# Delta rule, then a hash-routed mixture of experts: halves, fills and an order of loads

## The chip, the cores and the metric

The kernel runs on one core of a Trainium2 chip. The engines named here are TensorE (PE; its weight loads are PEld), VectorE (DVE), ScalarE (ACT), GpSimd (POOL) and SyncE (SP), which issues most DMAs. The metric is the device time of one execution in microseconds, lower is better.

## The reference

Two stages follow each other. The first is a delta rule over 4 batches, 8 heads, 768 steps and a head dimension of 48:

```python
k_n = k / (np.linalg.norm(k, axis=-1, keepdims=True) + 1e-06)
state = np.zeros((B, H, D, D))
for t in range(S):
    kt, vt, bt = (k_n[:, :, t], v[:, :, t], beta[:, :, t, None])
    y[:, :, t] = np.einsum('bhd,bhde->bhe', q[:, :, t], state)
    v_old = np.einsum('bhde,bhd->bhe', state, kt)
    state = state + bt[:, :, :, None] * np.einsum('bhd,bhe->bhde', kt, vt - v_old)
```

Its output, seen as 3072 tokens of 8 x 48 = 384 numbers, goes to the second stage. A hash of the token's id picks one of 8 experts, and each expert is a feed-forward layer with a ReLU between:

```python
expert_idx = token_ids * np.int64(2654435761) % np.int64(E)
for e in range(E):
    mask = expert_idx == e
    out[mask] = np.maximum(x[mask] @ w1[e], 0.0) @ w2[e]      # 384 -> 1024 -> 384
```

All numbers are float32.

## The kernel before

**Phase 1** works on 24 chunks of 32 steps (`NU`, `C`), with all batches and heads side by side. Four chunks make a group (`GC`). For each group the transposed keys and queries (`turn`, L457) give Gram matrices (`gram`, L483; `first_gram`, L525, for the first group). VectorE inverts them step by step: `inverse`, whose 31 steps are a product (L624) and a sum (L622), and which starts with a transpose of the Gram matrices (L584). `turn_back` (L638) transposes the result, and `spread_t` and `masks_of` make the stationary matrices `Tz` and `MT` out of it: on ACT (L550), or on DVE (L544) from chunk `LATE` = 20 on.

The chunks themselves are a chain, `chunk(c)`:

- `scale_v` makes V1 on DVE (L569).
- TensorE multiplies the state by the keys (`ask`, L659) into the PSUM bank `psX`. V1 minus this is R. Up to chunk 19 TensorE first puts -V1 into the bank (L690, with `minus`, a negated identity) and ACT copies the sum out with its sign turned (L695); from chunk 20 DVE subtracts (L699).
- `solve` (L709) multiplies R by Tz, and ACT copies the result, W, out (L723).
- `update` (L738) adds the keys times W to the state in the banks `psS`, and the state is copied to SBUF for the next chunk (`renew`: L762 on ACT, L764 on DVE).
- `answer` (L779) and a second `ask` with the queries make the chunk's rows in `psY`; ACT copies them out (L788), and POOL scatters them to `x_scratch` in DRAM, sorted by expert (`store`, L794).

From chunk `TAIL` on (20 of 0 to 23) a chunk is split: heads 0 to 3 stay in `psX`, heads 4 to 7 go to the bank `z1` (`zs[1]`), R and W are made in two parts, and the copy of the state is shared by ACT (batches 0 and 1) and DVE (batches 2 and 3).

**The order of the instructions** on each engine is fixed when the program is built. Each piece of work is a `task` with an engine, an estimated time, what it reads and writes, and the banks it claims. `order()` is a list scheduler: it walks through the tasks by estimated time and takes the ready one with the longest estimated rest. It also keeps an account of when TensorE's instructions are fetched, by counting their words:

```python
for m in range(issued // BLOCK, (issued + t["words"]) // BLOCK + 1):   # BLOCK = 256
    if m == len(begun):
        if m > 1:
            have = max(have, begun[-1])
            have += BUSY_FETCH if have < BUSY else FETCH               # 4600 or 3800 ns
        begun.append(max(s, have))
    s = max(s, begun[m])
```

Where it expects TensorE to be idle, `fill()` puts matmuls of the identity by itself into a bank that is unused when the gap begins (L1192), up to four blocks of 128 columns in one instruction, for gaps of over 380 ns in the first 80 us of the plan. Everything with its order fixed waits in it: a later instruction of an engine can't pass an earlier one that isn't ready.

**The first expert** (two blocks of 128 rows and a late one, `first_expert`: L1041, L1052, L1065, L1075) is scheduled by the same planner, as work for idle time. The late block's hidden values, `h_late`, lie in `xqs[0]`.

**Phase 2** goes through the other seven experts in the order `RANKS`. For each of them `fetch` asks SP for the rows (`load_x`, L100, and `load_numbers`, L104) into one of two tiles `xqs`, by turns; `turn` transposes them on DVE (L108); `gemm1` (L1226) has eight outputs that use four banks by turns and are evicted by ACT (L1229) and DVE (L1231) alternately; `gemm2_turned` (L1263) or `gemm2` (L1242) follows, and POOL scatters the result (L1252). Weights come by `load_w` (L94, L117) into a pool with two places, or for the second expert by `load_w_parts` (L94, L125). The transposes of the next expert's rows stand between the evictions of the present one. Before the loop SP is told: the second expert's rows, its weights, the third expert's weights, and the third expert's rows. Those rows go into `xqs[0]`, where `h_late` has been.

Of the kernel before, what the change touches and what calls it, by code (L numbers as in the profile page):

```python
# [13 lines left out]
ACT = mybir.ActivationFunctionType  # L14
# [6 lines left out]
def kernel(  # L21
# [11 lines left out]
    nc = tc.nc  # L33
    P = 128
    B, H, S, D = q.shape
# [13 lines left out]
    RANKS = [4, 0, 1, 2, 3, 5, 6, 7]  # L49
# [38 lines left out]
    def expert_at(rank, engine):  # L88
        return value(AT_E + rank, engine, E - 1)
# [21 lines left out]
    def load_w(e, pool, eng):  # L111
        s2 = moe_w2[bass.ds(e, 1)].rearrange("o f d -> (o f) d")
        w1_sb = pool.tile([P, CO, F], F32, name="w1_sb")
        for part in w1_parts(e, w1_sb, eng):
            part()
        w2_sb = pool.tile([P, FO, DIN], F32, name="w2_sb")
        eng.dma_start(out=w2_sb, in_=s2.rearrange("(fo p) d -> p fo d", p=P))  # L117
        return w1_sb, w2_sb
# [39 lines left out]

    with ExitStack() as phase1:
        NU = S // C  # L160
        TAIL = NU - 4
        GC = 4
        NG = NU // GC
        HU = H // 2
# [88 lines left out]
        def task(eng, ns, reads, writes, emit, words=0, kb=0, more=0, boost=0, job=None,  # L253
                 hold=0, claim=(), slack=0, idle=False, release=()):
            deps = {writer[r] for r in reads if r in writer}
            for w in writes:
                deps |= readers.get(w, set())
                if w in writer:
                    deps.add(writer[w])
            i = len(tasks)  # L260
            deps.discard(i)
            tasks.append(dict(eng=eng, ns=ns, deps=deps, emit=emit, words=words, kb=kb,
                              more=more, boost=boost, job=job, hold=hold,
                              claim=claim, slack=slack, idle=idle, release=release))
            for r in reads:
                readers.setdefault(r, set()).add(i)
            for w in writes:
                writer[w] = i
                readers[w] = set()
            return i  # L270
# [15 lines left out]
        def order():  # L286
# [33 lines left out]
            def fill(i, idle, at):  # L320

                nonlocal issued
                rate = 1.67
                if at < 2000:

                    rate, idle = 3.34, idle - 900
                idle = min(idle, 2750 if at < 2000 else 1100)
                while idle > FILL_OVER and at < FILL_UNTIL:
                    unused = [b for b in range(len(homes)) if banks[b] is not None
                              and banks[b] <= at]  # L330
                    if not unused:
                        break
                    n = min(4, max(1, int((idle - 160) / (rate * P))))
                    fills.setdefault(i, []).append((unused[0], n))
                    issued += 2
                    idle -= n * rate * P
                    at += n * rate * P
# [17 lines left out]
            while len(done) < n:  # L355
# [8 lines left out]
                at, e = best  # L364
# [307 lines left out]
        def chunk(c):  # L672
# [10 lines left out]
            if c == 0:  # L683
                R, r_names = V1, ("V10",) * 2
            else:
                R_, V1_ = [t.rearrange("p h d -> p (h d)") for t in (R, V1)]
                by_pe = c < LATE
                if by_pe:

                    task("PE", 680, (f"V1{c % 2}",), ("psX",), lambda: nc.tensor.matmul(  # L690
                        flats[0], lhsT=minus, rhs=V1_, start=True, stop=True,
                        skip_group_check=True), words=2)
                ask(c, 0, xs, xn, xc, by_pe)
                if by_pe:
                    task("ACT", 420, ("psX",), r_names, lambda: nc.scalar.activation(  # L695
                        R_, flats[0], ACT.Copy, scale=-1.0))
                for i, part in enumerate(wide if split else ()):
                    task("DVE", 320, (xn[i], f"V1{c % 2}"), (f"R{i}",),
                         lambda i=i, part=part: nc.vector.tensor_tensor(  # L699
                             R_[:, part], V1_[:, part], flats[i][:, part], op=ALU.subtract))  # L700
# [502 lines left out]
    with tc.tile_pool(name="w_pool2", bufs=2) as w_pool2, \  # L1203
# [79 lines left out]
        def fetch(e):  # L1283
            cols, cw, blocks, xq = own(e)
            row = value(AT_ROW + e, mybir.EngineType.SP, N)
            load_x(row, blocks, xq, nc.sync)
            xns[e] = m_i.tile([P, KT], F32, name="numbers")
            load_numbers(row, cols, cw, xns[e][0:cw, 0:cols, None], nc.sync)
# [13 lines left out]
        with tc.manual_schedule():  # L1302
            fetch(RANKS[1])
            for part in parts:
                part()
            w_tiles[2] = load_w(expert_at(RANKS[2], mybir.EngineType.SP), w_pool2, nc.sync)
            fetch(RANKS[2])
            n_ov = nc.values_load(ov_i[0:1, NOV:NOV + 1], min_val=0, max_val=NOV)
            for c in range(CO):
                turn(RANKS[1], c)  # L1310
            for k in range(SC):
                send_rows(o_first[:, k], idx_i[:, k:k + 1], True)
            send_rows(o_late, idx_i[:, SC:SC + 1], True)
            for i, e in enumerate(RANKS):
                if e == FIRST:
                    continue
                w1_sb, w2_sb = w_tiles.pop(i)
                rest = [e for e in RANKS[i + 1:i + 3]]
                done = RANKS[i - 1] if RANKS[i - 1] in oTs else None

                def between(fo):

                    to = max(3, i + 1)
                    if fo == 0 and to < E and to not in w_tiles:
                        w_tiles[to] = load_w(expert_at(RANKS[to], mybir.EngineType.SP),
                                             w_pool if to == 4 else w_pool2, nc.sync)
                    elif fo == 1 and len(rest) > 1:
                        fetch(rest[1])
                    if fo % 2 and fo // 2 < CO and rest:
                        turn(rest[0], fo // 2)  # L1330
                    if fo % 2 and done is not None:
                        send(oTs[done], done, fo // 2)

                h_sb = m_h.tile([P, FO, CAP], F32, name="h_sb")
                gemm1(w1_sb, xTs.pop(e), h_sb, CAPS[e], between)
                if KTS[e] > CO:
                    oTs[e] = m_t.tile([P, CO, CAP], F32, name="oT")
                    for j in range(CO):
                        gemm2_turned(w2_sb, h_sb, oTs[e], j, CAPS[e])
                else:  # L1340
                    cols, cw, _, _ = own(e)
                    for j in range(cols):
                        gemm2(w2_sb, h_sb, j, cw, idx[e][0:cw, j:j + 1], True)
# [49 lines left out]
```

## Time and profile before

| | before |
|---|---|
| timed runs, median (lowest to highest) | 505.26 us (505.12 to 509.08) |
| profiled execution, device time | 498.96 us |
| its span, first to last instruction | 497.4 us |
| mean granted TensorE clock | 0.970 |
| PE, DVE, ACT, POOL busy | 459.2, 228.8, 191.7, 71.6 us |
| chunk 0's first solve / chunk 20's / last answer's end | 50.73 / 205.06 / 224.06 us |
| second expert's first matmul | 255.29 us |

The profile is one execution. A busy time is the union of the engine's instructions; matmuls are pipelined and their ends are modelled, so that a TensorE that is shown as busy can still have a little room. The granted clock is a share of full speed. In a row of the instructions in order of time, the first number is the start, the second the length, and a bracket at the end tells how long the engine had been idle and what released it. Where instructions of several kinds are merged, xN counts them; a matmul of float32 shows as two records.

### The profile page before, as it was taken

To read this page: it belongs to the slowest core of one execution; us is meant where nothing else is said; L and a number is where in the kernel's file an instruction comes from. 1 tells how busy PE (TensorE), PEld (TensorE's weight loads), DVE (VectorE), ACT (ScalarE), POOL (GpSimd) and SP (SyncE) were. 2 spreads that over 40 slices of the span, in tenths; PEclk is the share of its full clock that TensorE was granted. 3 is DMA by queue.
4 is the path that set the end of the run, shared out by engine and by line. 5 is a ranking of instruction groups with operands and counts; after the bars stand their busy time and mean duration, and the time that the engine had idled before them with its cause. 6 is when DMAs were issued, how large, how long until landed. Compare 5 with 4: busy or idle time off the path is not lost. (4 is left out here: it accounts for less than half of the span.)

```text
span 497.4 us, 15828 instructions
## 1 busy us (share of the span) xinstructions
PE 459.2 (92%) x6648; PEld 312.5 (63%) x6648; DVE 228.8 (46%) x720; ACT 191.7 (39%) x443; POOL 71.6 (14%) x106
## 2 busy tenths in 40 slices
PE   8882899999899899899998999999999999999990
PEld 6762677787687777787754555555555565655650
DVE  5799979998998889850102013012021130110100
ACT  4762779988698687441221011011011110100100
POOL 6000101202020022320020012113011022001010
PEclk9996699999999899999999999999999999999996
DMA  9997756679444447523999995645543016401010
GB/s 137 170 154 116 114 112 132 131 151 189 99 101 100 100 112 176 151 72 77 186 271 246 244 222 140 152 129 114 112 151 73 0 39 164 144 7 39 0 31 15
DMA packets 137180, 60.61 MB, mean 122 GB/s; under 512 B 123005, under 2 KB 131825, under 8 KB 137108
## 3 DMA queue, kind: packets, MB, share of 16 engines
q1 hardware_dynamic: 131572, 49.80, 49.6%
q0 software_dynamic: 5344, 9.66, 6.1%
q8 instruction: 53, 0.87, 0.8%
q10 hardware_dynamic: 192, 0.12, 0.2%
q14 instruction: 19, 0.16, 0.1%
HBM read 49.19 MB, written 10.42 MB: 120 GB/s over the span
## 5 line engine op out<-in xcount | busy, mean ns | idle before, releaser
L1263 PE MATMUL bank<-h_sb,w_sb 128*128 128x424 f32 (+1 forms) x192 | 66.4, 506 | 0.0
L624 DVE TENSOR_TENSOR tmp<-U,Ni 128x87 f32<-128x87 f32 (+15 forms) x186 | 62.2, 339 | 3.2
L622 DVE TENSOR_TENSOR U<-U,tmp 128x87 f32<-128x87 f32 (+15 forms) x186 | 61.8, 338 | 2.9
L1252 POOL DMA_INDIRECT out_dram<-o_sb,tokens x25 | 29.3, 1172 | 199.2 <-ACT o_sb L1248 154.2
L1226 PE MATMUL z<-xT,w_sb 128*128 128x424 f32 (+3 forms) x168 | 57.4, 491 | 0.0
L1263 PEld LDWEIGHTS bank<-h_sb,w_sb 128*128 128x128 f32 x192 | 36.2, 190 | 28.4 <-issue 15.6
L794 POOL DMA_INDIRECT x_scratch<-x_sb,slot x24 | 24.8, 1031 | 183.0 <-ACT MT L550 50.5
L1231 DVE TENSOR_SCALAR h_sb<-z 128x424 f32<-128x424 f32 (+3 forms) x14 | 7.9, 562 | 88.5 <-PE z L1226 88.5
L1242 PE MATMUL bank<-w_sb,h_sb 128*121 128x384 f32 (+1 forms) x144 | 46.9, 486 | 0.0
L762 ACT ACTIVATE S<-psS 48x384 f32<-48x384 f32 (+1 forms) x92 | 42.7, 465 | 9.2 <-PE psS L738 7.9
L1226 PEld LDWEIGHTS z<-xT,w_sb 128*128 128x128 f32 x168 | 31.6, 190 | 22.2 <-issue 7.6
L1242 PEld LDWEIGHTS bank<-w_sb,h_sb 128*121 128x121 f32 (+1 forms) x144 | 26.6, 185 | 19.4
L779 PEld LDWEIGHTS psY<-W,MT 64*64 64x64 f32 x768 | 25.5, 138 | 11.1 <-issue 9.6
L1265 ACT COPY oT<-bank 128x424 f32<-128x424 f32 (+1 forms) x8 | 4.0, 499 | 72.9 <-PE bank L1263 72.9
L1226 PE MATMUL psY<-xT,w_sb 128*128 128x424 f32 (+3 forms) x84 | 30.0, 493 | 1.7 <-DVE h_sb L1231 1.7
L1248 ACT COPY o_sb<-bank 106x384 f32<-106x384 f32 (+3 forms) x14 | 6.7, 479 | 64.0 <-PE bank L1242 49.6
L779 PE MATMUL psY<-W,MT 64*64 64x48 f32 x768 | 29.1, 224 | 1.2 <-issue 1.2
L1226 PE MATMUL psX<-xT,w_sb 128*128 128x424 f32 (+3 forms) x84 | 29.9, 492 | 0.0
L738 PE MATMUL psS<-W,K 32*128 32x96 f32 x736 | 26.7, 280 | 2.5 <-ACT W L723 2.2
L738 PEld LDWEIGHTS psS<-W,K 32*128 32x128 f32 x736 | 22.7, 186 | 5.5 <-ACT W L723 3.6
L709 PE MATMUL psX<-R,Tz 64*64 64x48 f32 x672 | 25.2, 223 | 0.4 <-issue 0.2
L550 ACT ACTIVATE Tz<-TU,kmask 128x256 f32<-128x256 f32 x40 | 23.8, 716 | 3.7 <-DVE TU L638 3.7
(205 smaller groups left out, 665.6 us busy)
## 6 DMA issues: line engine op xcount, KB each, us to landing
w_sb<-in_moe_w_dram SPq DMA_DIRECT2D x32, 384.0 KB
w_sb<-in_moe_w_dram SPq DMA_DIRECT2D x6, 1536.0 KB
keys<-in_k_dram SPq DMA_DIRECT2D x24, 192.0 KB
Qt<-in_q_dram SPq DMA_DIRECT2D x24, 192.0 KB
V<-in_v_dram SPq DMA_DIRECT2D x96, 48.0 KB
K<-in_k_dram SPq DMA_DIRECT2D x96, 48.0 KB
wide<-in_moe_w_dram SPq DMA_DIRECT2D x8, 384.0 KB
xq<-x_scratch SPq DMA_DIRECT2D x12, 144.0 KB
```

Source lines behind the costliest of these rows:

```text
L550: lambda e=e: nc.scalar.activation(out[:, :, e].rearrange(order_of), in_.rearrange(order_of), ACT.Copy, scale=kmask[:, e:e + 1]))
L622: nc.vector.tensor_tensor(U[:, n:, 0:n], U[:, n:, 0:n], t, op=ALU.add)
L624: nc.vector.tensor_tensor(t, U[:, j:n, 0:n].to_broadcast([P, m, n]), Ni[:, j, n:, None].to_broadcast([P, m, n]), op=ALU.mult)
L709: nc.tensor.matmul(pws[i][rows, h], lhsT=Tz[rows, h].rearrange("p e i -> p (e i)"), rhs=R[rows, h], start=(h == (hs.start if split else 0) ...
L738: nc.tensor.matmul(state[0][:, b, 2 * D * u:2 * D * u + 2 * D], lhsT=K4[quarter(b), u].rearrange("p r d -> p (r d)"), rhs=W[quarter(b), 2 ...
L762: copy = nc.scalar.activation(put, get, ACT.Copy)
L779: nc.tensor.matmul(py[rows, h], lhsT=MT[rows, h].rearrange("p e i -> p (e i)"), rhs=W[rows, h], start=(c == 0 and h == 0), stop=True, skip ...
L794: put = nc.gpsimd.indirect_dma_start(out=x_dram[0:N, :], out_offset=bass.IndirectOffsetOnAxis(ap=slot[:, c:c + 1], axis=0), in_=x_sb, in_o ...
L1226: nc.tensor.matmul(h_ps[:, :width], lhsT=w1_sb[:, co, fo * P:(fo + 1) * P], rhs=xT[:, co, :width], start=(co == 0), stop=(co == CO - 1))
L1242: nc.tensor.matmul(o_ps[0:rows, 0:DIN], lhsT=h_sb[:, fo, col * rows:(col + 1) * rows], rhs=w2_sb[:, fo, :], start=(fo == 0), stop=(fo == F ...
L1252: scat = nc.gpsimd.indirect_dma_start(out=out[:, :], out_offset=bass.IndirectOffsetOnAxis(ap=idx, axis=0), in_=rows, in_offset=None, bound ...
L1263: nc.tensor.matmul(oT_ps[:, 0:width], lhsT=w2_sb[:, fo, i * P:(i + 1) * P], rhs=h_sb[:, fo, 0:width], start=(fo == 0), stop=(fo == FO - 1))
```

## The change

Four edits:

1. `TAIL` is `NU - 8`: chunks 16 to 23 are split, not 20 to 23.
2. For chunks that are split and have -V1 put in by TensorE (16 to 19), -V1 goes in by two matmuls, into the two banks, and ACT copies R out in two parts. The bank `z1` is claimed by chunk 16 on.
3. The cap on a gap that is filled is 3000 ns, not 1100, past the first 2000 ns of the plan.
4. SP is told to fetch the third expert's rows ahead of its weights.

```diff
-        TAIL = NU - 4
+        TAIL = NU - 8
...
-                idle = min(idle, 2750 if at < 2000 else 1100)
+                idle = min(idle, 2750 if at < 2000 else 3000)
...
                 by_pe = c < LATE
                 if by_pe:
 
-                    task("PE", 680, (f"V1{c % 2}",), ("psX",), lambda: nc.tensor.matmul(
-                        flats[0], lhsT=minus, rhs=V1_, start=True, stop=True,
-                        skip_group_check=True), words=2)
-                ask(c, 0, xs, xn, xc, by_pe)
-                if by_pe:
-                    task("ACT", 420, ("psX",), r_names, lambda: nc.scalar.activation(
-                        R_, flats[0], ACT.Copy, scale=-1.0))
-                for i, part in enumerate(wide if split else ()):
+                    for i, part in enumerate(wide if split else (slice(0, H * D),)):
+                        task("PE", 350 if split else 680, (f"V1{c % 2}",), (xn[i],),
+                             lambda i=i, part=part: nc.tensor.matmul(
+                                 flats[i][:, part], lhsT=minus, rhs=V1_[:, part], start=True,
+                                 stop=True, skip_group_check=True), words=2, claim=xc[i])
+                ask(c, 0, xs, xn, ((), ()) if by_pe else xc, by_pe)
+                for i, part in enumerate((wide if split else (slice(0, H * D),)) if by_pe else ()):
+                    task("ACT", 320 if split else 420, (xn[i],), r_names[i:i + 1] if split else
+                         r_names, lambda i=i, part=part: nc.scalar.activation(
+                             R_[:, part], flats[i][:, part], ACT.Copy, scale=-1.0))
+                for i, part in enumerate(wide if split and not by_pe else ()):
                     task("DVE", 320, (xn[i], f"V1{c % 2}"), (f"R{i}",),
...
+            fetch(RANKS[2])
             w_tiles[2] = load_w(expert_at(RANKS[2], mybir.EngineType.SP), w_pool2, nc.sync)
-            fetch(RANKS[2])
```

## The prediction

> **What bounds the kernel now.** I read the page's slices first, then the busy time by stage, then the order of instructions at the three places that the change touches. In the slices each digit is a tenth of 12.4 us:
>
> ```profile
> PE   8882899999899899899998999999999999999990
> DVE  5799979998998889850102013012021130110100
> PEclk9996699999999899999999999999999999999996
> ```
>
> VectorE is full from slice 2 to 17 and nearly idle after it; TensorE is full all through, except in slices 3 and 4, where its clock falls as well. The same by stage (us; busy time of PE, PEld, DVE, ACT, POOL; then clock and DMA):
>
> ```profile
> 16.00:60.00 44.00, 31.08 (x952) 23.30 (x949) 42.37 (x157) 26.77 (x79) 0.72 (x1) 0.81 0.88 136
> 60.00:176.80 116.80, 110.18 (x3222) 87.20 (x3226) 104.29 (x352) 97.26 (x219) 17.10 (x29) 0.99 0.58 121
> 176.80:198.84 22.04, 20.57 (x589) 16.22 (x593) 20.17 (x56) 16.86 (x36) 5.18 (x8) 1.00 0.71 161
> 198.84:224.00 25.16, 23.85 (x737) 20.33 (x733) 17.07 (x36) 11.42 (x30) 7.31 (x10) 1.00 0.41 111
> 224.00:488.00 264.00, 259.48 (x866) 154.77 (x864) 36.64 (x83) 31.82 (x70) 33.20 (x29) 1.00 0.50 120
> ```
>
> Until 60 VectorE's first inverse sets the pace (42.4 busy of 44). From 60 to 199 the chunks and the inverses hold each other: VectorE has 104 of 117, then 20.2 of 22. From 199 the chunks run alone, and from 224 the experts keep TensorE busy without a break but one. A microsecond won on the chunks counts only where VectorE has room for it.
>
> **Part 1, longer fills.** A fill multiplies the identity into a free bank while the planner thinks TensorE idle; the change lifts the cap on one gap from 1100 to 3000 ns. At 1.67 ns a column, a gap at the old cap holds one fill of four blocks of 128 columns (855 ns); at 3000 it holds 4+4+4+1, nine blocks more. Only fills of four can grow; past the first gap (whose cap stays) the trace has three, at 11.15, 26.12 and 52.61.
>
> The one at 11.15 (1.13 us, so 0.28 a block) stands before the last quarter of the first gram, ahead of the inverse. The code's count of instruction words passes 512 there, and the planner lets that block begin 4.6 us after the one before, which begins with the second quarter (8.39 in the trace): 12.99, so a gap of 1.8 us after 11.2. The new cap fits three more blocks, 0.85 us; the trace shows an issue stall of 0.38 us right behind (12.48 to 12.86) that they hide. **+0.5 us**; bounds 0 and 9 x 0.28 - 0.38 = 2.1.
>
> The one at 26.12 costs nothing: TensorE waits 1.99 us at 38 and 6.32 us before 50.73. Without this cover it would be at most 2.5.
>
> The third is here:
>
> ```profile
> 50.73 1.95 PE L709 MATMUL psX<-V,Tz 64*64 64x48 f32 x32 [6.32 <-DVE V L569]
> 52.61 2.07 PE L1192 MATMUL psY<-ident 128*128 128x512 f32 x2
> 54.47 1.49 PE L690 MATMUL psX<-V,minus 128*128 128x384 f32 x2
> 55.89 1.84 PE L779 MATMUL psY<-W,MT 64*64 64x48 f32 x32
> 57.66 1.15 PE L738 MATMUL psS<-W,K 32*128 32x96 f32 x32
> ```
>
> The fill runs at half clock (2.07 against 1.13) and already overshoots: W, which the next matmuls need, was copied out by 53.22. Behind it wait L690, L779 and L738, and on L738 the whole chunk chain. A block costs 0.52 here. Nine cost 4.7; the clock returns at about 57.2 in either case, so what is pushed past that runs at full speed and about 2.4 comes back: +2.3. None cost 0. The planner's gap is its lag plus W's copy (250+390+150 = 790 ns) plus what ACT still does; a fill of four says at least 1015, growth starts at 1235. I take two blocks: **+0.5 us**.
>
> A rule speaks for this edit. The Trainium skill (TensorE: Matmul & The Clock Gate, "HAM oscillation") says that an idle gap of over about 3.4 us drops TensorE to half clock, so gaps should be filled. The trace agrees: clock 0.50 from 42 to 56, round the gap of 6.32 us. By the rule the four rows from 50.73 would cost 1.13, 1.13, 0.91 and 1.13 instead of 7.35 us: -3.05. But the row shows no fill in that gap, although it is longer than the old cap: the cap isn't what kept it out. A fill needs a bank that is free when the gap begins, and the grams just before have filled the banks. By the row the gain is 0, and I take that.
>
> **Part 2, eight chunks by halves.** Chunks 16 to 19 join 20 to 23: R and W in two parts in psX and z1, and the state's copy shared by ACT and DVE. They keep the negated V1 on TensorE. Today a chunk ends as in the first row, and the first split chunk solves at the second:
>
> ```profile
> 194.85 1.15 PE L738 MATMUL psS<-W,K 32*128 32x96 f32 x32 [0.59 <-ACT W L723]
> ...
> 205.06 0.67 PE L709 MATMUL psX<-R,Tz 64*64 64x48 f32 x16
> ```
>
> Chunks 17 to 19 take 6.37 us each (the ends of L738), with TensorE busy 5.78; chunks 21 and 22 take 5.2, but without L690's 0.91 us. So what halves can win is the 0.59 us wait for W, four times: -2.3, no more, because TensorE is then full. The state's copy:
>
> ```profile
> L762 ACT ACTIVATE S<-psS 48x384 f32<-48x384 f32 x20 | 9.7, 484 | 3.4 <-PE psS L738 3.1
> L764 DVE COPY S<-psS 48x192 f32<-48x192 f32 x12 | 4.2, 352 | 2.6 <-PE psS L738 2.4
> L762 ACT ACTIVATE S<-psS 48x192 f32<-48x192 f32 x12 | 3.9, 324 | 3.5 <-PE psS L738 3.3
> ```
>
> ACT's four copies of 484 become four of 324: 0.64 us saved. DVE gets four of 352 a chunk, 1.48 us from first to last; four chunks make 5.9. They fall on the last inverse, while DVE is busy 20.2 of 22 us, and chunk 20 needs its result:
>
> ```profile
> 198.84 1.25 DVE L638 STREAM_TRANSPOSE TU<-U 128x1024 f32<-128x1024 f32 x1
> 200.19 1.03 DVE L544 TENSOR_TENSOR Tz<-TU,kmask 128x512 f32<-128x512 f32 x1
> ```
>
> Tz is ready at 201.22 and used at 205.06: 3.84 us of slack. 5.9 - 3.84 = **+2.1 us**: VectorE is late at chunk 20, and what TensorE won before is waited away. Bounds: -2.3 if the copies find idle time, +3.5 if each chunk's copies also stand 0.35 us in DVE's order before the state is there (behind them wait the inverse and V1). Holding z1 from chunk 16 costs nothing: the grams are over by 170, and the first expert's matmuls begin at 223.99.
>
> **Part 3, rows ahead of weights.** The third expert's rows go to a tile that the first expert's late block uses, so SP can't ask for them before 255.46. Today its weights are issued in that time (243 to 249.5), and the rows queue behind them. DVE stands in order before a transpose of the rows, and the evictions behind it hold TensorE's banks:
>
> ```profile
> SPq L100 <- PE bank L1075: 5.1, 1, 5.1
> ```
>
> ```profile
> 270.89 0.65 DVE L108 STREAM_TRANSPOSE xT<-xq 128x448 f32<-128x448 f32 x1 [10.46 <-DMA xq<-x_scratch]
> ```
>
> ```profile
> 272.08 2.40 PE L1226 MATMUL psY<-xT,w_sb 128*128 128x424 f32 x6 [1.68 <-DVE h_sb L1231]
> ```
>
> After: four row DMAs and the numbers take 2.4 us of SP (as at 232.7 to 235.2) and land some 3.6 us after the last, as the second expert's did: about 261, before the eviction due at 264. The 1.68 us go: **-1.7 us**, on the path. Everything behind the rows' wait on SP moves: weights issued from 258 instead of 243, 3.1 MB at some 250 GB/s, there by 271, needed at 289.7; the fourth expert's weights by 284 (needed at 325) and its rows by 287 (needed at 294). POOL's queue isn't touched. The thinnest cover is 7 us; if it went, the stall of 1.7 would come back one expert later.
>
> **Sum.** +0.5 + 0.5 + 2.1 - 1.7 = +1.4 us: 498.96 becomes 500.4. The timed runs of before have a median of 505.26, 6.3 above the profiled one; carried over, **506.7**.
>
> **Rivals.** A change of under 1% (5 us) is about what a measurement of this kernel can't tell from none.
> - *The fills set the end (slower).* If the planner's gaps reach 3000, the fills at 11.15 and 52.61 get all nine blocks: 2.1 + 2.3, up to 4.7 if the clock comes back no sooner. For it: the third fill already overshoots. Against: the waits worked out above are below 2 us. 4.4 to 6.8, with the other parts (+0.4): about 511.2. With all nine and the clock back at 57.2 it is 4.8, just under 1%; it is over from the point where the clock comes back later.
> - *The halves pay.* VectorE's copies fit, and chunks 16 to 19 keep the 2.3: -2.3 + 1.0 - 1.7 = -3.0, 502.3. For it: VectorE waited 1.2 us before V1 at 176.8. Against: 0.2 from there to 198.84.
> - *The clock stays up.* The rewritten order frees a bank before 50.73: -3.05 and the rest +1.4, 503.6; with the halves paying too, 499.2.
> - *Phase 1 keeps its pace.* No fill grows on the path and the slack holds: -1.7, 503.6.
>
> **Chances.** Forecast 0.40, fills 0.22, halves 0.20, clock 0.10, rows alone 0.08. The planner writes the whole order anew, which can move any case by 2 or 3 us. Over 1% slower: 0.13 of the fills' case and 0.05 of the forecast; over 1% faster: 0.11, from halves, clock and both. The range goes from just short of those two together (500) to the fills' case near its bound (511.8).
>
> **What would show it.** Right: in the stage before chunk 20, DVE L764 copies among the inverse, TU about 4 us later, and chunk 20's first solve waiting for Tz; more L1192 records at 11 and 53; the wait of DVE on the rows under 2 us and no TensorE wait at 272. Wrong: L1192 in the gap before 50.7 and a clock of 1.0 there; chunks 16 to 19 at 5.8 us with chunk 20 not held; any TensorE wait on weights after 289.

## The result and the profile after

| | before | after |
|---|---|---|
| timed runs, median (lowest to highest) | 505.32 us (505.12 to 509.08) | 501.56 us (500.29 to 502.11) |
| profiled execution, device time | 498.96 us | 501.32 us |
| its span | 497.4 us | 499.7 us |
| chunk 20's first solve / last answer's end | 205.06 / 224.06 us | 208.34 / 228.37 us |

The changed kernel is faster: ratio 0.9899 [0.9857, 0.9941]. The forecast was 506.7 us and slower than before. Two more batches of runs gave 0.9863 [0.9811, 0.9916] and 0.9921 [0.9899, 0.9943]. (Ratios leave out disturbed runs of the kernel before, so that they can differ a little from the ratio of the medians.)

The table contradicts itself. By the two profiles the changed kernel is 2.4 us *slower*, near the +1.4 that was forecast for the profiled execution; by the timed runs it is 3.8 us faster. The experiments below show why: these two profiles were not taken under the same conditions. In the one after, the sixteenth update of the state ends at 179.91 us, 4.0 later than in the one before (175.95). Where both kernels were profiled under like conditions (batch 3 below) it ends 3.7 us earlier, not later: at 175.15 against 178.86. So times in the first two profiles are to be read from that update on, not from the start.

In the third expert's start (260 to 300 us) TensorE is busy without a break; in the kernel before it was busy for 38.33 of 40 us:

```profile
260.00:300.00 40.00, 40.00 (x116) 21.51 (x115) 6.08 (x12) 4.41 (x9) 2.84 (x4) 1.00 1.06 235
```

The start of chunk 20, VectorE's rows and then TensorE's:

```profile
203.01 1.25 DVE L638 STREAM_TRANSPOSE TU<-U 128x1024 f32<-128x1024 f32 x1
204.29 1.04 DVE L544 TENSOR_TENSOR Tz<-TU,kmask 128x512 f32<-128x512 f32 x1
205.34 1.48 DVE L767 COPY S<-psS 48x192 f32<-48x192 f32 x4
206.85 1.05 DVE L544 TENSOR_TENSOR Tz<-TU,kmask 128x512 f32<-128x512 f32 x1
207.93 0.35 DVE L702 TENSOR_TENSOR R<-V,psX 128x192 f32<-128x192 f32 x1
```

```profile
208.34 0.67 PE L712 MATMUL psX<-R,Tz 64*64 64x48 f32 x16 [0.61 <-DVE R L702]
```

VectorE holds chunk 20, as the forecast said: a copy of the state stands between the two parts of Tz, R comes behind both, and the solve waits for R. But TU is not late. It stands at 203.01 where it was at 198.84, and of these 4.2 us the sixteenth update accounts for 4.0: TU begins 23.1 us behind it, and began 22.9 behind it before.

### The profile page after: what moved, and what is told of

It reads as the page before. It is cut to its first block, busy times and chain, and to the rows that moved or that the text cites. A ratio compares the mean times of both kernels' runs of the same rounds, so it can differ in the third digit from the quotient of the medians.

```text
span 499.7 us, 15899 instructions
## 1 busy us (share of the span) xinstructions
PE 464.8 (93%) x6662; PEld 316.7 (63%) x6662; DVE 232.9 (47%) x736; ACT 189.8 (38%) x451; POOL 70.9 (14%) x106
## 5 line engine op out<-in xcount | busy, mean ns | idle before, releaser
L622 DVE TENSOR_TENSOR U<-U,tmp 128x87 f32<-128x87 f32 (+15 forms) x186 | 61.7, 338 | 2.5
L1266 PEld LDWEIGHTS bank<-h_sb,w_sb 128*128 128x128 f32 x192 | 36.2, 190 | 28.4 <-issue 15.6
L797 POOL DMA_INDIRECT x_scratch<-x_sb,slot x24 | 24.6, 1026 | 188.0 <-DVE U L622 46.9
L765 ACT ACTIVATE S<-psS 48x384 f32<-48x384 f32 (+1 forms) x92 | 40.1, 436 | 12.6 <-PE psS L741 11.4
L741 PE MATMUL psS<-W,K 32*128 32x96 f32 x736 | 28.3, 281 | 1.4 <-ACT W L726 0.8
L741 PEld LDWEIGHTS psS<-W,K 32*128 32x128 f32 x736 | 23.7, 186 | 5.1 <-issue 2.1
L1234 DVE TENSOR_SCALAR h_sb<-psY 128x424 f32<-128x424 f32 (+3 forms) x14 | 7.9, 565 | 40.5 <-PE psY L1229 40.5
```

The lines of the kernel that those rows point to most:

```text
L622: nc.vector.tensor_tensor(U[:, n:, 0:n], U[:, n:, 0:n], t, op=ALU.add)
L741: nc.tensor.matmul(state[0][:, b, 2 * D * u:2 * D * u + 2 * D], lhsT=K4[quarter(b), u].rearrange("p r d -> p (r d)"), rhs=W[quarter(b), 2 ...
L765: copy = nc.scalar.activation(put, get, ACT.Copy)
L797: put = nc.gpsimd.indirect_dma_start(out=x_dram[0:N, :], out_offset=bass.IndirectOffsetOnAxis(ap=slot[:, c:c + 1], axis=0), in_=x_sb, in_o ...
L1234: nc.vector.tensor_scalar(out=h_sb[:, fo, :width], in0=h_ps[:, :width], scalar1=0.0, scalar2=None, op0=ALU.max)
L1266: nc.tensor.matmul(oT_ps[:, 0:width], lhsT=w2_sb[:, fo, i * P:(i + 1) * P], rhs=h_sb[:, fo, 0:width], start=(fo == 0), stop=(fo == FO - 1))
```

## The experiments

The kernels ran in five batches (the expectations say "call"); those of one batch share a chip and the runs of the kernel before. Line numbers differ by a few between the kernels.

**Batch 1: the parts alone, and the kernel before against itself.** Edits: none; the rows only; the fills only; the halves only.

```diff
+            fetch(RANKS[2])        # e1_rows
             w_tiles[2] = load_w(expert_at(RANKS[2], mybir.EngineType.SP), w_pool2, nc.sync)
-            fetch(RANKS[2])
...
-                idle = min(idle, 2750 if at < 2000 else 1100)   # e2_fills
+                idle = min(idle, 2750 if at < 2000 else 3000)
...
-        TAIL = NU - 4              # e3_halves, with edit 2 of the change
+        TAIL = NU - 8
```

> The kernel before, unchanged, run as if it were a new one. The timed runs of before (505.1 to 509.1) lie 6 us above its profiled execution (499.0), so first the question is what it does from run to run. If the 499 was only one lucky execution with the same order, some runs here are again near 499 and most near 505, and the granted clock of the slow ones is below 0.970 (clock theory: about 0.955, some 3 windows of 3.4 us more at half clock). If the gap is not the clock, the clock is 0.970 in all of them.

> Only the third expert's rows ahead of its weights; phase 1 keeps its instruction order to the letter. All theories: 1.7 us less than before (ratio 0.9966) in the same state, no TensorE wait near 272, DVE's wait for the rows under 2 us. If it brings the whole 3.7 us of the change, the prediction mis-sized the stall.

> Only the cap of 3000 ns. The planner's order changes with it. Prediction: 1.0 us more than before. Clock theory: the longer fills (and what they move) spare half-clock windows, 2 to 4 us less than the timed median of before, clock above 0.970. Theory of the order: some us either way, without a change in the clock.

> Only the eight chunks by halves. Prediction: 2.1 us more, VectorE late at chunk 20 (Tz ready near 205.5, not 201.2). Clock theory: no help for the first 60 us, so 505 to 507 as before. Theory of the order: some us either way, with the first chunks' pace changed too.

Measured, with the median of before at 501.24 (59 runs, 496.78 to 505.8): before again 501.24, ratio 0.9986 [0.995, 1.0021]; rows 498.41, 0.9979 [0.9955, 1.0003]; fills 500.07, 0.9987 [0.9961, 1.0013]; halves 500.71 (one of 14 runs took 1552 us), 0.9981 [0.9948, 1.0014]. So no part alone gives anything that can be told from none, and the kernel before spreads over 9 us by itself. My first reading was that the -3.8 us were the luck of four runs. That was wrong, as the next batch showed.

**Batch 2: the change again, the change without its rows, a filled gap, and fills in the old order.**

```diff
             def solve(i, hs):
+                for n in (4, 3) if c == 0 and i == 0 else ():     # e6_warm_rows
+                    nc.tensor.matmul(psY.rearrange("p (n x) -> p n x", n=4)[:, 0:n],
+                                     lhsT=ident, rhs=ident[:, None, :].to_broadcast([P, n, P]),
+                                     start=True, stop=True, skip_group_check=True)
...
+                most = 0 if at < 2000 else min(idle, 3000)        # e7_fills_same
                 idle = min(idle, 2750 if at < 2000 else 1100)
...
+                    most -= n * rate * P
+                    at += n * rate * P
+                while i in fills and most > FILL_OVER and at < FILL_UNTIL:
+                    n = min(4, max(1, int((most - 160) / (rate * P))))
+                    fills[i].append((unused[0], n))
+                    most -= n * rate * P
```

e6 has the rows ahead as well. In e7 the blocks are added to gaps that have a fill already, and the planner doesn't count them, so its order stays.

> The changed kernel itself, timed again with many more executions of both kernels. If the first -3.7 us was mostly the luck of which executions of the kernel before were drawn (their times follow the granted clock), the ratio is now 0.995 to 0.999, that is 0.5 to 2.5 us below the kernel before. If the whole -3.7 us is the change's own, the ratio is 0.990 to 0.994. If the prediction's sum (+1.4 us) holds on average, it is 1.002 to 1.004. In the profile the last answer should again end 2 to 4 us later than in the kernel before (224.06) and the stretch behind it be 1 to 2 us shorter than 261.1.

> Longer fills and halves in eight chunks, the third expert's rows back behind its weights. If the rows bring the gain, this is 1.5 to 2.5 us above the changed kernel of the same call and at or above the kernel before (0 to +1.4 us). If the fills and halves bring it, it is as fast as the changed kernel. VectorE should again wait some 10 us for rows of the third expert.

> The kernel before with the rows ahead, and two fills (4 and 3 blocks) issued straight ahead of the first chunk's first solve, in the 6.3 us gap in which TensorE waits for the first inverse. By the clock rule (the gap puts the clock to half, some 3.05 us are lost behind it) the half-clock stretch that begins at about 50 goes or is shorter by one window of 3.4 us, and the time is 1.5 to 3 us below the kernel with the rows alone (about 495.5 to 497 where that one had 498.6). If the fills themselves delay the first solve or the clock is set by the lighter work ahead of the gap too, the half-clock stretch stays at 42 to 57 and the time is that of the rows alone or up to 1 us more.

> The kernel before with every instruction in its order, only the idle stretches filled with the blocks that the higher cap would give. It tells the fills' own cost from that of the rewritten order. By the prediction the fills cost +0.5 us ahead of the first gram and +0.5 us at 52.6, so +0.5 to +1 us. By the clock rule longer fills keep the clock up and give -1 to -3 us. If the order was what moved the chunks 4 and 5 in the changed kernel, their updates end here where the kernel before has them (88.0 and 94.9 plus the fills' own 0.5 to 1).

Measured, with before at 507.93: the change 501.63 (0.9863 [0.9811, 0.9916]); without its rows 501.69 (0.9864 [0.9812, 0.9915]); filled gap and rows 504.23 (0.9921 [0.9891, 0.995]); fills in the old order 507.17 (0.9979 [0.9954, 1.0004]). The kernel before is 7 us slower here than in batch 1 at the same granted clock (means 0.968 and 0.967), the change is where it was. The gain is real, and fills with halves have all of it here. Fills alone in the old order bring nothing in this batch, fills alone in their own order and halves alone brought nothing in batch 1.

In e6 the gap ahead of chunk 0 is closed and the clock is back at 49.7, not at 56.1; the first update ends at 55.7, not at 58.2. That is 2.5 of the 3.05 us which the prediction worked out by the rule on idle gaps (compared with e7, the same batch). But in that profile the clock is at half again from 131.6 to 138.4 and from 199.9 to 206.7, and at the end 3.7 us are won, rows included.

**Batch 3: the kernel before, profiled beside the change.** The edits are those above.

> The kernel before, profiled and timed beside the changed kernel on one chip. So far its executions lay at 496.8 to 505.8 us in one call and 504.3 to 512.6 in another, at the same granted clock (0.95 to 0.976), while the changed kernel was at 500.3 to 502.5 in both of its calls. If a stall that differs from chip to chip makes the kernel before late, its profile here shows it: more waits of TensorE put down to issue, above all in the first stage, 2 to 7 us more than the 2.4 us of the first profile (between 58 and 225), whenever its time is over 503. If it is the clock alone, the profile shows more half-clock windows of 3.4 us and no more issue.

> The changed kernel in the same call. If it doesn't have what differs from chip to chip, it is at 500 to 503 us again, whatever the kernel before is: 0.985 to 0.995 of it where that is over 505, and 0.998 to 1.004 where that is at 501.

> Only the halves in eight chunks, in the same call. Timed once at 500.5 us beside 501.1 of the kernel before. If the halves take away what makes the kernel before late on some chips, it stays at 500 to 502 here; if the combination of longer fills and halves does, it follows the kernel before (within 1 us of it).

> Only the third expert's rows ahead of its weights, in the same call; first-stage order and instructions are those of the kernel before. It should stay 1.5 to 2.5 us below the kernel before wherever that lies, since it changes only the stall of 1.7 us at 272. If the kernel before is at 505 to 508 here, this one is at 503 to 506.

Measured, with before at 500.44: before again 501.99, 1.0034 [0.9995, 1.0072]; the change 494.97, 0.9921 [0.9899, 0.9943]; halves 500.17, 1.0008 [0.9986, 1.0029]; rows 499.14, 0.9984 [0.9954, 1.0014]. Now the change is at 495, 6.7 us below its time in batch 2, as the kernel before is 7.5 below its own. Both kernels have two levels, and all that was measured in one batch was at one of them. This batch gives the comparison that the first two profiles could not: both kernels at the lower level. First TensorE's longest waits between 58 and 225 (line waited for: total, times, longest), of the kernel before:

```profile
PE psX L659 <- issue: 2.5, 1, 2.5
PE psS L738 <- ACT W L723: 2.2, 5, 0.6
PE z L483 <- issue: 1.5, 2, 0.9
```

and of the changed one:

```profile
PE psX L659 <- ACT S L765: 1.5, 4, 0.5
PE psY L782 <- issue: 1.1, 2, 0.7
```

The waits for W are gone, and so is a stall of 2.5 us in which TensorE waited for nothing that the profile shows; behind that stall (160.2 to 162.8) the clock of the kernel before is at half from 164.1 to 174.3. (That stall is not in every execution of the kernel before: in its first profile the longest put down to issue in this stretch is 0.8 us.)

Then why do the halves alone bring nothing? TensorE's rows of one of the newly split chunks (start, length, line, operation), first with the halves alone:

```profile
188.29 0.67 PE L712 MATMUL psX<-R,Tz 64*64 64x48 f32 x16
188.89 0.54 PE L659 MATMUL psY<-S,KQ 128*32 128x96 f32 x16
189.36 0.67 PE L712 MATMUL z<-R,Tz 64*64 64x48 f32 x16
189.96 0.70 PE L741 MATMUL psS<-W,K 32*128 32x96 f32 x16
190.59 0.59 PE L692 MATMUL psX<-V,minus 128*128 128x192 f32 x2
191.11 0.70 PE L741 MATMUL psS<-W,K 32*128 32x96 f32 x16
```

Then in the changed kernel, with the same work:

```profile
191.07 0.63 PE L712 MATMUL psX<-R,Tz 64*64 64x48 f32 x16
191.53 0.63 PE L712 MATMUL z<-R,Tz 64*64 64x48 f32 x16
192.10 0.87 PE L659 MATMUL psY<-S,KQ 128*32 128x96 f32 x32
192.90 1.15 PE L741 MATMUL psS<-W,K 32*128 32x96 f32 x32
193.97 0.43 PE L692 MATMUL psX<-V,minus 128*128 128x192 f32 x1
```

TensorE waits for nothing in either fence. From start to start, sixteen matmuls of L712 take 0.60 us where another kind follows and 0.46 where their own kind does; the update takes 1.26 us in two groups (0.63 each; the row after the last one shown begins at 191.74) and 1.07 in one. This chunk is 6.57 us with the halves alone (190.59 to 197.16, L692 to L692) and 5.87 in the changed kernel (188.10 to 193.97). Over chunks 16 to 19 the line changes 40 times with the halves alone and 29 times in the changed kernel, but the gain over all four is smaller than this one chunk suggests. They take 25.8 us (e10; e3: 26.4) against 24.4, and 0.9 of the difference is no gain: 32 matmuls that answer chunk 15's queries (L659, `psY<-S,wide`) stand behind the sixteenth update in the old order and ahead of it in the new. On equal work it is 0.5 to 1.1 us.

The larger difference is on VectorE. These are the products of the last inverse that are still to do between the sixteenth update's end and TU: for the kernel before (e8, 178.86 to 201.75 us), the halves alone (e10, 178.08 to 203.49) and the changed kernel (e9, 175.16 to 198.16), and for the last one also the copies of the state in that stretch (count, then busy us and mean ns of one):

```profile
L624 DVE TENSOR_TENSOR tmp<-U,Ni 128x156 f32<-128x156 f32 (+15 forms) x26 | 9.4, 361 | 0.9
```

```profile
L624 DVE TENSOR_TENSOR tmp<-U,Ni 128x220 f32<-128x220 f32 (+15 forms) x22 | 8.0, 364 | 0.6
```

```profile
L624 DVE TENSOR_TENSOR tmp<-U,Ni 128x240 f32<-128x240 f32 (+15 forms) x20 | 7.2, 359 | 0.6
L767 DVE COPY S<-psS 48x192 f32<-48x192 f32 x12 | 4.3, 356 | 1.1 <-PE psS L741 0.9
```

With the sums (L622) the inverse still needs 19.1 us in e8, 16.0 in e10 and 14.4 in e9. So the changed order has done 4.7 us more of it beforehand, and the copies (4.3 us ahead of TU) take that place: TU begins 23.0 us behind the sixteenth update, and 22.9 in e8. With the halves alone it begins 25.4 (e3: 25.9) behind it, and TensorE then loses what the chunks had won: from the 20th update to the 23rd 18.0 us (e3: 17.8) against 17.1 in the changed kernel and 16.7 in the kernel before.

**Batch 4: is it the place in the code?** The stalls put down to issue sit at like places of TensorE's stream: in the first profile of before the five such gaps of over 0.15 us behind the first update end where the count of matmuls and weight loads, modulo 256, is 145 to 153, 1.3 to 1.7 us after a block of code had landed. (The Trainium skill, Runtime: NRT & Kernel Launch, "Instruction fetch mechanics", has code come in blocks of 256 instructions, its fetch mostly hidden; the profile agrees on the blocks, 53 of them with 0.87 MB, and here the fetch isn't always hidden.) The change adds instructions and so moves all that follows. The edit shifts the stream alone:

```diff
                 for b, n in fills.get(i, ()):
+                    if start[i] > 2000 and n > 2 and cuts:    # cuts: 1 in a, 2 in b
+                        for k in range(0, n * P, 16):
+                            nc.tensor.matmul(homes[b][:, k:k + 16], lhsT=ident,
+                                             rhs=ident[:, k % P:k % P + 16], ...)
+                        cuts.pop()
+                        continue
```

> The kernel before, in its order, with none of the three edits; one fill of 4 blocks ahead of the first stage is issued as 32 matmuls of 16 columns, so TensorE's instructions behind it lie 62 further in their stream. If the stalls of TensorE put down to issue sit at fixed places of the stream (in the first profile all of those of 0.3 us and more began where the count of matmuls and weight loads, modulo 256, was 145 to 193, 1.3 to 2.9 us after a block of code had landed), they move to other instructions, and the time changes by 1 us or more either way, with another share of half-clock windows. If the code's place has nothing to do with it, the time is that of the kernel before within 1 us (the fill itself may take 1 us more).

> As the last, with a second fill cut up, 124 instructions of shift in all. By the theory of the code's place: another time, 1 us or more away from the kernel before or from the shift by 62; a kernel with none of the edits as fast as the changed one (ratio 0.988 to 0.992) would show that the changed kernel's gain can be had from the place alone. By the theory that the edits bring the gain in themselves: within 1 us of the kernel before.

> The changed kernel, in its order, one fill of 4 blocks cut up likewise: 62 instructions of shift. By the theory of the code's place it loses part of its gain: ratio 0.994 to 1.000, and a half-clock window comes back behind 130. By the theory that the edits bring the gain in themselves it stays at 0.986 to 0.992, the clock full from about 57 to the end.

> The changed kernel with two fills cut up, 124 instructions of shift. Expectations as for the last: 0.994 to 1.000 by the code's place, 0.986 to 0.992 by the edits themselves.

Measured, with before at 508.83: 522.94 and 529.39 for the kernel before, shifted; 515.67 and 526.13 for the changed one, ratios 1.0284, 1.04, 1.0146 and 1.0366. As a test by time it failed: a fill so cut takes some 11 us (10.99 and 11.95 in the two profiles of shift b), since 32 matmuls of float32 are 64 records and as many weight loads: all four ratios carry 12 to 25 us of delay ahead of the first update, and the shift was twice the one that I had counted. The stage behind the first update is unharmed and can be compared: to the last update it takes 167.0 and 169.4 us in the kernel before and 165.8 and 164.2 in the changed one, which took 163.9 without a shift (e4). The place in the code may be worth 1 or 2 us; it doesn't turn the one kernel into the other.

This batch and batch 2 also show what the upper level is. Inside a solve, in the kernel before of batch 4 (POOL scatters an answer meanwhile):

```profile
208.68 0.98 POOL L794 DMA_INDIRECT x_scratch<-x_sb,slot  x1 [5.59 <-ACT MT L550]
...
208.74 1.02 PE L709 MATMUL psX<-R,Tz 64*64 64x48 f32 x28
...
209.99 0.33 PE L709 MATMUL psX<-R,Tz 64*64 64x48 f32 x4 [0.22 <-issue]
...
210.36 0.49 ACT L723 ACTIVATE W<-psX 128x384 f32<-128x384 f32 x1 [1.29 <-PE psX L709]
```

The same in batch 3, at the lower level:

```profile
196.03 1.14 PE L709 MATMUL psX<-R,Tz 64*64 64x48 f32 x32
...
197.22 0.49 ACT L723 ACTIVATE W<-psX 128x384 f32<-128x384 f32 x1 [0.86 <-PE psX L709]
```

The scatter's instruction ends at 209.66, TensorE pauses at 209.76 in mid-solve and goes on at 209.99. W's copy begins 1.62 us behind the solve's start, where it was 1.19; a chunk of the old order (17 and 18) is 6.81 us long there, where it was 6.37. I count gaps of over 0.1 us between two like matmuls that lie within a scatter or up to 0.6 us behind its end: 9 to 14 in each of the eleven profiles of the changed kernel's first run and of batches 2, 4 and 5, and 0 to 3 in each of the nine of batches 1 and 3 and of the first profile of before. So the first profile of before is of the lower level, and the first one of the change of the upper. The gaps counted add up to 2.4 to 4.1 us in a profile of the upper level, less than the 7 us between the levels; as in the solve above, what hangs on a pause can lose more than the gap that is seen. In the order of before the pauses fall into the solve, on the chain of the chunks; in the changed order mostly elsewhere: TensorE's waits for issue ahead of the solves of psX in this stage are 2.5 us in ten pieces in the kernel before of batch 4, and 0.8 in three in the changed one.

**Batch 5: are the halves needed, and a faster version.** Edits: the change without edits 1 and 2; the change with the two fills of e6 ahead of the first solve.

> Longer fills and rows ahead, halves in four chunks as before. Sum of the parts timed alone: -0.8 (fills) and -1.5 to -2.5 (rows), so 2.3 to 3.3 us below the kernel before (0.993 to 0.995). If the planner's order with the longer fills is what brings the gain, it is as fast as the changed kernel: 0.986 to 0.990. If that order needs the halves too, it stays at the sum of the parts or above it.

> The changed kernel with two more fills (4 and 3 blocks) straight ahead of the first chunk's first solve. The same fills in the kernel before brought the clock back at 49.7 and not at 56.1 and ended the first update at 55.7 and not at 58.2, but other half-clock windows followed. The changed kernel had no such window behind 57 in four of its profiles, so the 2.5 us should stay: 2 to 3 us below the changed kernel, ratio 0.980 to 0.987. If the windows come whenever the first one is filled, there is one behind 130 and the ratio is 0.987 to 0.993.

Measured, with before at 509.08: fills and rows 507.53, 0.9975 [0.994, 1.001]; the change with the filled gap 501.60, 0.9847 [0.9798, 0.9895]. Without the halves the gain is gone. The filled gap can't be told from the change alone (0.9863 in its own batch at that level). In its profile the two fills run from 47.1 to 50.5, and yet the clock is at half until 55.9 and the first update ends at 58.2; in e6 the same fills had brought it back at 49.7. What sets this apart stays open. One difference is on record: the changes of the clock lie multiples of some 3.4 us apart in each profile (32.6, 36.1, 42.9, 49.7 in e6; 32.0, 35.4, 42.3, 55.9 in e17), and counted in such steps the fills begin 0.4 us into a step in e6 and 1.4 us into one in e17. No run tests whether that decides it.

The stages in the profiles, from the ends of the state's updates (us; half clock counted behind the first update's end):

| kernel | first update ends | to the 16th | 16th to last (23rd) | first to last | last to TensorE's end | half clock |
|---|---|---|---|---|---|---|
| *lower level:* before, first profile | 58.8 | 117.1 | 42.9 | 160.0 | 266.3 | 3.4 |
| before, e0 / e8 | 57.9 / 57.8 | 120.1 / 121.1 | 43.2 / 43.1 | 163.3 / 164.2 | 265.2 / 266.2 | 10.2 / 10.2 |
| rows, e1 / e11 | 58.2 / 58.1 | 116.5 / 117.5 | 43.3 / 45.2 | 159.7 / 162.7 | 264.4 / 264.4 | 0 / 3.4 |
| fills, e2 | 59.1 | 117.3 | 43.9 | 161.2 | 265.1 | 6.8 |
| halves, e3 / e10 | 58.1 / 57.9 | 119.6 / 120.2 | 44.2 / 43.7 | 163.8 / 163.9 | 265.4 / 264.4 | 10.2 / 6.8 |
| **changed, e9** | 58.9 | 116.2 | 41.6 | 157.8 | 264.4 | 0 |
| *upper level:* rows and filled gap, e6 | 55.7 | 122.9 | 49.9 | 172.7 | 264.8 | 13.6 |
| fills in the old order, e7 | 58.2 | 119.8 | 46.6 | 166.5 | 264.9 | 0 |
| before, shifted, e12 / e13 | 70.0 / 81.2 | 120.5 / 123.0 | 46.5 / 46.4 | 167.0 / 169.4 | 267.6 / 264.8 | 0 / 3.4 |
| fills and rows, e16 | 58.1 | 119.8 | 50.7 | 170.5 | 264.3 | 6.8 |
| **changed, first / e4** | 58.4 / 58.2 | 121.5 / 121.1 | 42.8 / 42.9 | 164.4 / 163.9 | 264.8 / 264.8 | 0 / 0 |
| changed without rows, e5 | 58.0 | 120.7 | 42.8 | 163.6 | 264.8 | 0 |
| changed, shifted, e14 / e15 | 71.4 / 82.8 | 123.0 / 121.4 | 42.8 / 42.8 | 165.8 / 164.2 | 264.8 / 264.8 | 0 / 0 |
| changed with filled gap, e17 | 58.2 | 122.3 | 43.0 | 165.3 | 264.8 | 0 |

The old orders have 0.9 us of work behind the 16th update that the changed one has ahead of it, so that 0.9 of each difference in the third column is no gain. From the first update to the last TensorE has the same work in both but for a few records (4387 in e8, 4395 in e9), and at each level every profile with fills and halves (one of each run) is ahead of every other: 157.8 against 159.7 to 164.2 us, and 163.6 to 165.8 against 166.5 to 172.7. Against the profiles without half clock alone it is 157.8 against 159.7, and on average 164.5 against 166.8.

## Why the prediction was wrong, step by step

**The step that failed is the +2.1 of part 2:** "VectorE is late at chunk 20, and what TensorE won before is waited away". It set 5.9 us of copies of the state against 3.84 us of slack and took VectorE's order as it was. The slack was smaller than read: the solve reads both parts of Tz, and the second was ready at 202.76, 2.3 us ahead of the solve:

```profile
201.73 1.03 DVE L544 TENSOR_TENSOR Tz<-TU,kmask 128x512 f32<-128x512 f32 x1
```

That alone would have made the forecast worse. What turned it round is that the copies don't come on top. In the changed order 4.7 us more of the last inverse are done when the sixteenth update ends, and TU begins 23.0 us behind that update as against 22.9. VectorE makes 28 copies where it made 12, and chunk 20 waits for VectorE; but only the last chunk's copies (1.48 us between the two parts of Tz) are in its way. From the update of chunk 19 to the first solve of chunk 20 it is 3.9 us, and was 2.7: **1.2 us, where the forecast had chunk 20 lose 4.4** (the 2.3 won before and 2.1 more). By the end of the last update the loss is 0.5 (17.1 against 16.7 us from the 20th to the 23rd, e9 and e8).

*What TensorE wins* was put at 2.3 us at most for chunks 16 to 19. At the lower level they take 24.4 us (e9) against 26.4 (e1); without the 0.9 that was only moved, that is -1.1. (Chunks 17 to 19 take 6.1, 5.9 and 5.6 us; 5.8 stood in the forecast as a sign that it was wrong.) At the upper level it is 24.6 against 28.4 (e4 and e12), or -2.9 on equal work, since the pauses leave the chain as well. That level was not in any profile I had. So the stage from the 16th update on has some -0.6 us (41.6 plus 0.9 against 43.1) or -2.8 (42.8 plus 0.9 against 46.5), where +2.1 stood. The bounds, -2.3 to +3.5, held the first and not the second; "no more, because TensorE is then full" took TensorE's time as a constant, and the two fences of one chunk show that it isn't (6.57 and 5.87 us at no wait).

With the halves alone the forecast's mechanism is there: TU is 2.5 to 3.0 us later behind the 16th update, and the stage is 0.5 to 1.1 us longer (43.7 and 44.2 against 43.1 and 43.2). The working was near for the edit and wrong for the change.

**The order was held fixed.** The working priced each edit in the old order and gave the planner's new one "2 or 3 us" either way. Of TensorE's 6650 matmul records over 900 stand at another place in the list. At the lower level the new order loses in the middle (the changed kernel's fifth update ends at 89.8 in e9, before's at 87.0 in e8) and wins it back ahead of the 16th (e9 is through the 15th and 16th chunk in 14.4 us, e1 in 16.6). In sum the stretch to the 16th update is there as fast as in the old order without half clock (116.2 against 116.5 and 117.5, e1 and e11), and up to 4.9 us faster than in the old order with it. At the upper level it is 1.6 us slower on average (120.7 to 123.0, against 119.8 to 120.5 without half clock there), and the gain lies behind the 16th. Which of the edits brings what is known only in part: fills and rows without halves have nothing of the gain at the upper level (e16), but the halves without fills were run only at the lower one. There the ratios of the parts alone multiply to 0.996, uncertain by 0.004, against 0.992 for the change, so that even there the parts may have more of the gain than they showed.

**The clock stays up** was the rival at 0.10, for another place: a fill in the gap before 50.7. That didn't happen (the gap is 6.07 us in the first profile after, the clock at half from 42 to 56), and the weighing of rule and row was right as far as it went. But the row was read with too much trust in the rule: the clock is at half from 40.4 on in the first profile of before, and the gap opens only at 44.41. The gap can have kept the clock down; it did not bring it down. What happened is behind it: none of the seven profiles of the changed order (with e5, the shifts and e17) has half clock behind the first update, ten of the other thirteen have 3 to 14 us of it. Over the timed runs of batch 3 the mean granted clock is 0.973 against 0.967 to 0.969, and 0.01 goes with 2.3 to 3.5 us in those runs of before (without and with the longest of them), so that this is worth some 1 to 2 us. The windows are rarer in the changed order, not surely gone: three of its 17 timed runs there are at 0.967 or 0.968, below its unshifted profiles (0.973 to 0.977). That a stall sets a window off is likely from e8 and e0 (a stall of 1.2 us ends at 131.1, half clock begins at 131.2), but one of 1.45 us in the first profile after set off none, and no run takes a stall away alone: argued, not shown.

**Part 1 was right where it forecast a loss.** The first update ends 0.9 us later in the two lower-level profiles with longer fills than in the seven without (59.0 against 58.1, which spread from 57.8 to 58.8); +1.0 stood there. But most of it is the first fill: it grew from 1.13 to 2.42 us, and the first solve begins 0.7 us later (51.2 against 50.5). The one that was to bring the other half, at 52.89, kept its four blocks and its 2.07 us. So the sum was met by luck. At the upper level it ends at 58.0 to 58.4 with them; without them no kernel was profiled there that wasn't changed ahead of it.

**Part 3 was right in mechanism.** VectorE's wait for the rows fell from 10.46 to 1.59 us, TensorE has no wait from 260 on and none on weights to the end. But the stall that goes isn't always 1.68: without the rows the stretch behind the last update took 264.4 to 266.3 us in the lower-level profiles, with them 264.4 in all three. That is -1.0 on average; at the upper level the change without rows is as fast as with them (264.8 both).

**The level.** I carried 6.3 us from the profiled execution to the timed runs as a constant. The profile was of the lower level. The timed runs beside it, at 505.12 and more, fit the upper one, whose lowest in batch 2 was 504.33, as the change's 501.56 fits its upper level (501.63 in batch 2, 494.97 in batch 3); no profile of those runs of before shows it. Sums on top of that number compare unlike things, and so would a reading of the first two profiles against each other. That 501.56 lies between 500 and 511.8, where the prediction expected it, is luck for the same reason.

Within batch 3 the sum is, e8 to e9, +1.1 (first update), -4.9 (to the 16th: clock, stall, order), -1.5 (to the last, 0.9 of it moved work), -1.8 (rows): -7.1 us of span, 500.4 to 493.3. That e8 had more half clock than most makes it larger than the ratio's -4.0. At the upper level, where the change was first timed, the 6.3 us of batch 2 (507.93 to 501.63) are 2 to 3 us between the first update and the last in profiles without half clock (164.5 against 166.8) and, by the timed clock of 0.974 against 0.968, an estimated 2 us of half clock at 2.3 to 3.8 us for 0.01; the rest is not accounted for.

## What to carry to other kernels

When a change makes a planner write the order anew, price the order and not the edit: here copies that would have made VectorE 2.5 to 3 us late found their place because the new order had done 4.7 us more of the inverse beforehand. Before two profiles are set against each other, or a profile's sum is carried to timed runs, profile the old kernel again beside the new one, and read times from an event that both have, not from the start: 4.0 of the 4.2 us by which TU seemed late had arisen ahead of the 16th update, in profiles of different levels. And time taken from VectorE's slack should be followed to the instruction that waits: 5.9 us of copies cost 1.2 there and 0.5 at the stage's end.

## What the runs showed of the hardware

- **Two levels by the batch.** The same kernel before had medians of 501.24, 507.93, 500.44, 508.83 and 509.08 us in five batches, at a like clock (means 0.967 to 0.969). At the upper level TensorE pauses for 0.1 to 0.5 us, seldom more, beside or behind GpSimd's scatters. The chip of batch 3, at the lower level, was by its number that of batch 5, at the upper. What decides the level stays open.
- **Half clock comes back behind dense work.** With TensorE 94% busy (110.2 of 116.8 us in the first profile of before), stretches of 3.4, 6.8 or 10.2 us at half clock appear at 131 to 142, 160 to 176 or 196 to 207 in some executions and not in others. The Trainium skill (TensorE: Matmul & The Clock Gate, "HAM oscillation") speaks of idle gaps of over about 3.4 us; the longest stalls seen ahead of these are of 0.6 to 2.5.
- **Changing the kind of matmul costs in the solves.** Sixteen matmuls of a solve take 0.46 to 0.50 us from start to start ahead of their own kind and 0.56 to 0.60 ahead of another (e9 and e10, 150 to 225 us). The products of state and keys (L659) don't show it: 0.44 to 0.47 ahead of another kind in e10, 0.35 to 0.56 ahead of their own.
